# A new order of steps, all stores on SyncE and wider empty matmuls in an RWKV-5 attention with a squared-ReLU feed-forward

## The chip, the core and the metric

The kernel runs on one core of one Trainium2 chip. Its metric is the device time of one execution in microseconds (us). In this kernel TensorE (PE) does matrix products into the accumulators in PSUM, VectorE (DVE) and ScalarE (ACT) work element by element and read those accumulators, GpSimd (POOL) works element by element on data in SBUF and issues some DMAs, and SyncE (SP) only issues DMAs. Each engine works through its own list of instructions in order; waits between engines are semaphores.

## What is computed

The input is r, k, v of shape [4 batches, 8 heads, 768 steps, 48], a decay w and a bonus u per head and channel, and two feed-forward weights, [384, 2048] and [2048, 384]. Per head a state of 48 x 48 runs over time, and its output, with the heads side by side, goes through a feed-forward with a squared ReLU:

```python
for t in range(S):
    cur = einsum('bhd,bhe->bhde', u * k[t], v[t])
    y[t] = einsum('bhd,bhde->bhe', r[t], state + cur)
    state = w * state + einsum('bhd,bhe->bhde', k[t], v[t])
x = y.transpose(0, 2, 1, 3).reshape(B * S, H * D)      # 3072 x 384
out = square(maximum(x @ w_in, 0)) @ w_out             # 3072 x 384
```

## The kernel before

The 3072 rows are cut into 24 chunks of 128 rows. Chunk i belongs to batch i % 4 and is the (i // 4)th of its batch, so chunks 0 to 3 begin the four batches. Inside a chunk the recurrence is written as matrix products with powers of the decay (tables Wkhat and Wt2) on k and r; between chunks it goes through a state per batch (S0W). The steps of chunk i, with their names in the order list:

- `ld.r.i`, `ld.k.i`, `ld.v.i` load 192 KB each. `rh`, `kh` scale r and k to bf16 (lines 338, 335); `P0`, `P1`, `du`, `dv` make the bonus term (341, 345, 348, 353); `vb` casts v.
- Scaled r and k are turned, either by PE (`T`, line 362, copied out by `Tc` on ACT) or by a DMA transpose on SP (`XB`, line 368).
- `A` (line 375) makes the scores, `Bm` (383) masks them, `Y` (391, 393) makes the chunk's output in PSUM, `xs` (410) adds the bonus, `U` (402) is the chunk's share of the state, `S0`, `ts`, `S` (417, 420, 423) update the state.
- The result is turned again, by PE (`X`, 428, copied by `xTc`) or by DMA (`xX`, 435).

The chunks form 13 groups, 0 and 1 with one chunk, 2 to 12 with two (chunks 4 and 5 are group 2, and so on). The feed-forward works on a group: `F1.g.s` (line 444) is one PSUM bank of the first product for group g, `re` (452 on ACT, 454 on DVE) the ReLU of that bank, `sq` (459 on ACT; 461 or 463 on DVE) its square, `F2.i.q` (471) a quarter of the second product for chunk i, and `os.i` and `out.i` (503) copy and store its result. `F1` uses two PSUM banks in turn. `F2c` (485) is the second product of chunk 22 alone, in two halves of columns.

The weights come in pieces. Of w_in there are eight (W1_0 to W1_7, 384 KB each): `lW.0.s` loads piece s into one of four staging buffers wsa (line 323), `cW.0.s` casts it to bf16, on ACT (259) or POOL (261). Piece 2 comes by `W.0.2`, a DMA from POOL that casts on its way (332), and so do the four pieces of w_out (`W.1.q`). A bank `F1.g.s` of groups 0 and 1 needs pieces 2s and 2s+1: `F1.0.2` needs pieces 4 and 5.

`Z.n.b` (line 494) issues n empty matmuls on the identity into bank b, while PE has no data yet.

The whole order is written out by hand in ORDER: one entry per step, `name.indices:engine/buffers`. The program walks through the list once and issues each step on the engine named (P, A, D, G for POOL, S for SP). So the order of the entries of one engine is that engine's program order, and the choice of engine and of buffers stands there too. A step waits for what it reads and for the last readers of the buffer it writes; SP and POOL hold back everything behind a DMA that waits.

## Time and profile before

| what | value |
|---|---|
| median of 3 runs | 174.68 us (174.6 to 174.76) |
| the profiled execution itself | 175.31 us |
| its span, first to last instruction | 173.5 us |
| granted TensorE clock | 1.00 of full speed over the span |
| PE busy | 162.7 us (94%), 1805 matmuls |
| DVE, ACT, POOL busy | 127.8 us, 118.0 us, 91.2 us |
| HBM read and written | 20.46 MB, 4.72 MB |

The span starts with the first instruction of the program; 1.8 us of the profiled execution lie outside it. In rows of the timeline the first number is the start in us from the beginning of the span, the second the duration; "x24" says how many instructions are merged, and the brackets give the idle time before the first of them with what ended it. In groups by line the numbers behind the bar are the busy time, the mean duration of one in ns, and the idle time of the engine before them. Rows of waits give the total, the number of waits and the longest one. Rows on a DMA queue give packets, megabytes and the share of the 16 DMA engines' time. A DMA issue tells how long its queue's sequencer was held and, in the list of issues, the median time until the data had landed.

### The profile page before, as it was taken

How to read it: one execution, taken by the hardware profiler on the slowest of the kernel's cores; microseconds unless marked ns; L12 is line 12 of the kernel's file. 1: busy time of each engine (PE TensorE's matmuls, PEld its weight loads, DVE VectorE, ACT ScalarE, POOL GpSimd, SP SyncE). 2: the span in 40 equal slices, each digit the busy share in tenths (PEclk: the TensorE clock that was granted, in tenths of full speed). 3: DMA queues.
4: the chain of work that ended last, by engine and by line, in shares of the span. 5: the costliest groups of instructions: out<-in, count | busy, mean ns of one | idle time of the engine just before them, and what ended most of it. 6: DMA issues, size and time to landing. Idle time of an engine off the chain costs nothing.

```text
span 173.5 us, 4580 instructions
## 1 busy us (share of the span) xinstructions
PE 162.7 (94%) x1805; PEld 126.7 (73%) x1805; DVE 127.8 (74%) x241; ACT 118.0 (68%) x220; POOL 91.2 (53%) x113
## 2 busy tenths in 40 slices
PE   3979579999999999999999999999999999999992
...
GB/s 98 221 240 278 195 244 194 196 211 215 140 229 210 203 236 154 230 211 178 201 216 173 238 127 183 204 133 209 193 232 135 95 37 26 159 0 91 49 62 74
DMA packets 104788, 29.14 MB, mean 168 GB/s; under 512 B 98008, under 2 KB 104288, under 8 KB 104768
## 3 DMA queue, kind: packets, MB, share of 16 engines
...
q10 hardware_dynamic: 152, 0.14, 0.2%
...
HBM read 20.46 MB, written 4.72 MB: 145 GB/s over the span
## 4 chain that ended last, share of the span: by engine, by line
PE 76%; DMA 11%; SPq 8%; issue 1%; ACT 1%; POOL 1%; DVE 0%; POOLq 0%; ACTq 0%
PE bank L471 33%; PE bank L444 31%; DMA ldk<-in_k_dram 7%; SPq L319 7%; DMA wsa<-in_moe_w_in_dram 3%; PE bank L375 3%; PE bank L393 2%; PE bank L391 2%; PE bank L402 2%; SPq L323 2%; PE bank L485 2%; PE bank L428 1%; PE bank L362 1%; ACT rkT L259 1%; POOL urow L217 0%
## 5 line engine op out<-in xcount | busy, mean ns | idle before, releaser
L444 PE MATMUL bank<-xT,W 128*128 128x256 bf16 (+1 forms) x624 | 74.0, 264 | 1.7 <-POOL W L261 1.3
L471 PE MATMUL bank<-W,hq 128*128 128x384 bf16 x368 | 69.9, 326 | 0.0
L444 PEld LDWEIGHTS <-W 128*128 128x128 bf16 x624 | 55.6, 98 | 12.2 <-POOL W L261 1.6
L452 ACT ACTIVATE hr<-bank 128x512 bf16<-128x512 f32 x78 | 45.7, 596 | 25.6 <-PE bank L444 24.5
L471 PEld LDWEIGHTS <-hq 128*128 128x128 bf16 x368 | 34.5, 98 | 17.6 <-DVE hq L461 0.3
L459 ACT ACTIVATE hq<-hr 128x512 bf16<-128x512 bf16 x77 | 45.6, 625 | 1.9 <-DVE hr L454 1.7
L383 DVE TENSOR_TENSOR Bm<-bank,maskJT 128x512 bf16<-128x512 f32 x48 | 31.0, 681 | 2.7 <-PE bank L375 2.1
L454 DVE TENSOR_SCALAR hr<-bank 128x512 bf16<-128x512 f32 x18 | 12.3, 689 | 16.0 <-PE bank L444 15.9
L345 POOL TENSOR_TENSOR P<-P,ub 128x384 f32<-128x384 f32 x16 | 17.5, 1095 | 12.4 <-DVE P L341 12.3
L341 POOL TENSOR_TENSOR P<-ldr,ldk 128x384 f32<-128x384 f32 x14 | 14.3, 1027 | 11.4 <-DMA ldr<-in_r_dram 6.1
L410 DVE TENSOR_TENSOR xs<-bank,dv 128x384 bf16<-128x384 f32 x24 | 12.8, 549 | 4.9 <-PE bank L393 2.7
L338 POOL TENSOR_TENSOR rk<-ldr,Wt 128x384 bf16<-128x384 f32 x12 | 12.1, 1013 | 7.7 <-DMA ldr<-in_r_dram 7.6
L335 POOL TENSOR_TENSOR rk<-ldk,Wkhat 128x384 bf16<-128x384 f32 x10 | 10.5, 1061 | 7.5 <-DMA ldk<-in_k_dram 5.4
L348 DVE TENSOR_REDUCE du<-P 128x8 f32<-128x384 f32 x24 | 12.9, 543 | 1.6 <-POOL P L345 1.5
L353 POOL TENSOR_TENSOR dv<-ldv,du 128x384 f32<-128x384 f32 x14 | 12.3, 882 | 3.2 <-DVE du L348 3.2
L259 ACT COPY os<-bank 128x384 f32<-128x384 f32 (+1 forms) x17 | 7.9, 473 | 8.0 <-PE bank L471 4.7
L494 PE MATMUL bank<-identity 128*128 128x128 bf16 x139 | 10.4, 240 | 2.7 <-POOL identity masks.py:199 2.7
L494 PEld LDWEIGHTS <-identity 128*128 128x128 bf16 x139 | 9.4, 110 | 2.9 <-POOL identity masks.py:199 2.7
L393 PE MATMUL bank<-vb,Bm 128*128 128x48 bf16 x192 | 10.9, 183 | 0.2 <-ACT xT L259 0.2
L259 ACT CAST vb<-ldv 128x384 bf16<-128x384 f32 x16 | 8.1, 508 | 4.1 <-DMA ldv<-in_v_dram 4.1
L375 PE MATMUL bank<-rkT 48*128 48x128 bf16 x192 | 8.2, 218 | 2.5 <-ACT rkT L259 1.7
L259 ACT COPY rkT<-bank 128x1024 bf16<-128x1024 bf16 x7 | 7.1, 1011 | 4.4 <-PE bank L362 4.4
(64 smaller groups left out, 174.7 us busy)
## 6 DMA issues: line engine op xcount, KB each, us to landing
ldk<-in_k_dram SPq DMA_DIRECT2D x24, 192.0 KB, 3.8
ldr<-in_r_dram SPq DMA_DIRECT2D x24, 192.0 KB, 3.7
ldv<-in_v_dram SPq DMA_DIRECT2D x24, 192.0 KB, 4.0
...
out_dram<-os SPq DMA_DIRECT2D x13, 192.0 KB, 3.0
out_dram<-os POOLq DMA_DIRECT2D x10, 192.0 KB, 3.2
...
rkT<-rk SPq DMA_TRANSPOSE x17, 3.7
```

Source lines behind the costliest of these rows:

```text
L259: e.copy(o, a)
L341: e.tensor_mul(P0b[slot[f"P{i}"]], loaded("r", i), loaded("k", i))
L345: e.tensor_mul(t, t, ub)
L348: e.tensor_reduce(dub[slot[f"dv{i}"]], P0b[slot[f"P{i}"]], axis=mybir.AxisListType.X, op=ALU.add)
L375: e.matmul(heads(bank(f"bA{i}{h}"), 128)[:, hc, :], t[p0 : p0 + D, HP + hc, :], t[p0 : p0 + D, hc, :], start=True, stop=True, skip_group_c ...
L383: e.tensor_mul(Bmb[slot[f"Bm{i}{h}"]], heads(bank(f"bA{i}{h}"), 128), mask_b)
L393: e.matmul(y[:, hc, D * h : D * (h + 1)], m[h][:, hc, :], vb[:, 2 * hc + h, :], start=(c == 0), stop=True, skip_group_check=True,)
L444: e.matmul(hp[:, fi, :], W1[f // 2][:, c, 128 * (f % 2) : 128 * (f % 2 + 1)], xt[:, c, :], start=(c == 0), stop=(c == CCH - 1), skip_group ...
L452: e.activation(hr, hp, AF.Relu)
L459: e.activation(hq, hr, AF.Square)
L471: e.matmul(bank(f"bO{i}", "bO")[:, 0:d_model], hqb[slot[f"hq{g},{f // m}"]][:, at : at + L], W2[q][:, f % 4, :], start=(f == 0), stop=(f = ...
L494: e.matmul(banks[b][:, 0:128], identity, identity, start=True, stop=True, skip_group_check=True)
```

## The change

ORDER is written anew from its first entry to its last, with the same steps. Three more things differ: all 23 whole-chunk stores are issued by SP (ten came from POOL before), `ld.v.3` is issued by POOL instead of SP, and the empty matmuls are issued four at a time as one matmul of 512 columns. What the order list holds up to the second product of the early groups, and at its end:

```diff
-ld.k.2:S/0 w:A tab:A shw:D ld.k.1:S/1 u:S ld.r.1:S/0 Z.48.4:P Z.4.5:P logw:A Wk:A/0 kh.1:D/0 ld.k.0:S/2 P0.1:D/0 WtS:A
-ld.r.0:S/1 Wt:A/1 rh.1:D T.1:P/0 kh.0:D/1 P0.0:G/1 shu:D P1.1:G ld.r.2:S/2 P0.2:G/2 Z.8.4:P ld.k.3:S/3 rh.0:D kh.2:D/2
-ld.r.3:S/3 Tc.1:A/0 rh.2:D P1.0:G Z.16.5:P P0.3:G/3 kh.3:D/3 T.2:P/1 A.1:P/2/3 du.1:D/0 ld.v.1:S/0 Z.13.4:P vb.1:G/0
-Bm.1.0:D/0 Tc.2:A/1 rh.3:D Z.6.5:P T.0:P/0 Bm.1.1:D/1 Tc.0:A/2 ld.v.0:S/1 du.0:D/1 A.0:P/2/1 T.3:P/3 WkS:A vb.0:G/1
-Z.6.4:P Bm.0.1:D/2 Y.1:P/0 Z.22.5:P lW.0.6:S/0 dv.1:G dv.0:G lW.0.0:S/1 Bm.0.0:D/3 wc:S xs.1:D/0 cW.0.6:A lW.0.1:S/2
-lW.0.7:S/3 A.2:P/1/2 Z.16.4:P Bm.2.1:D/4 P1.2:G P1.3:G ld.v.2:S/2 cW.0.1:G cW.0.0:A du.2:D/2 cW.0.7:G Tc.3:A/3 X.1:P/0
-du.3:D/3 Y.0:P/2 xs.0:D/1 xTc.1:A/0 dv.2:G ld.v.3:S/3 vb.2:A/2 A.3:P/3/2 X.0:P/0 vb.3:A/3 WLcol:A Bm.3.0:D/5 Bm.2.0:D/0
-xTc.0:A/1 F1.1.3:P/1 W.0.2:G U.1:P/3 re.1.3:A/0 F1.1.0:P/0 Y.2:P/1 Bm.3.1:D/1 re.1.0:A/1 lW.0.5:S/0 W.1.0:G dv.3:D
-lW.0.4:S/2 Y.3:P/0 xs.3:D/2 F1.0.0:P/1 xs.2:D/3 lW.0.3:S/1 cW.0.5:A W.1.1:G F1.0.3:P/0 X.3:P/2 re.0.0:A/2 sq.1.0:A0/0
-X.2:P/0 xTc.3:A/0 cW.0.4:G U.2:P/1 re.0.3:D/3 W.1.2:G F1.0.2:P/1 cW.0.3:G WLm:G ld.r.4:S/4 F1.1.2:P/0 xTc.2:A W.1.3:G
...
+Z.48.4:P w:A ld.r.0:S/0 ld.r.1:S/1 tab:A shw:D Z.8.5:P u:S ld.k.1:S/0 Z.13.4:P shu:D ld.v.1:S/0 ld.k.0:S/1 P0.1:D/0
+ld.k.2:S/2 Z.6.5:P logw:A P0.0:G/1 Wk:A/0 kh.1:D/0 Wt:A/1 P1.1:D rh.1:D kh.0:D/1 T.1:P/0 Tc.1:A/0 rh.0:D ld.r.3:S/2
+Z.16.4:P T.0:P/1 A.1:P/2/3 ld.v.0:S/1 ld.k.3:S/3 vb.1:A/0 kh.2:D/2 du.1:D/0 rh.3:D/3 Bm.1.1:D/0 Tc.0:A/1 vb.0:A/1
+A.0:P/0/3 kh.3:D ld.r.2:S/3 rh.2:D lW.0.1:S/0 ld.v.2:S/2 Z.22.5:P T.3:P/1 Tc.3:A/2 T.2:P/1 P1.0:G Bm.0.0:D/1 wc:S
+lW.0.7:S/1 Bm.1.0:D/2 dv.1:G Y.1:P/0 Z.16.4:P du.0:D/1 P0.2:G/2 P0.3:G/3 xs.1:D/0 Tc.2:A/3 X.1:P/2 Bm.0.1:D/3 P1.2:G
+vb.2:A/2 A.2:P/0/1 cW.0.7:A Bm.2.0:D/4 A.3:P/3/0 lW.0.6:S/2 cW.0.1:G Bm.2.1:D/5 ld.v.3:G/3 du.2:D/2 xTc.1:A/0 Z.4.5:P
+W.0.2:G dv.0:G dv.2:G Y.0:P/1 P1.3:G Bm.3.0:D/2 Bm.3.1:D/0 Z.6.4:P cW.0.6:A F1.1.3:P/1 vb.3:G/3 xs.0:D/1 Y.2:P/2 X.0:P/3
+lW.0.0:S/3 lW.0.5:S/1 re.1.3:D/0 cW.0.0:A W.1.0:G lW.0.4:S/0 lW.0.3:S/2 du.3:D/3 WtS:A W.1.1:G ld.r.4:S/4 xTc.0:A/1
+xs.2:D/2 WLcol:A cW.0.4:G F1.1.0:P/0 F1.0.3:P/1 Y.3:P/0 U.1:P/1 re.1.0:A/1 dv.3:D X.2:P/3 ld.k.4:S/4 cW.0.5:A xs.3:D/3
+ld.r.5:S/5 F1.0.0:P/0 X.3:P/2 re.0.3:A/2 sq.1.0:A0/0 re.0.0:D/3 xTc.3:A/0 WLm:G ld.k.5:S/5 sq.0.3:D2/1 xTc.2:A
+sq.0.0:D2/2 U.0:P/0 sq.1.3:D2/3 F1.0.2:P/1 re.0.2:A/4 ld.k.7:S/6 F1.1.2:P/0 re.1.2:A/5 F1.2.1:P/1 ld.v.4:S/4 re.2.1:A/1
...
-F2.21.2:P F2.20.0:P/0 re.12.2:A/2 sq.12.2:D2/29 F1.12.5:P/1 F1.12.4:P/0 F2.21.3:P re.12.5:D/0 out.19:S re.12.4:D/4
-os.21:D/3 sq.12.1:D2/6 F1.12.7:P/1 sq.12.3:A0/3 sq.12.6:A0/5 F2.20.1:P re.12.7:A/2 F2.23.0:P/1 sq.12.7:D1/8 F2.23.1:P
-out.21:S sq.12.5:A0/2 F2.20.2:P out.17:G F2.20.3:P sq.12.4:D2/0 F2.23.2:P os.20:A/1 F2.23.3:P F2c.22.1:P/0 os.23:A/3
-out.20:S out.10:G F2c.22.0:P/1 os.22.0:A/0 out.22.0:A os.22.1:D out.23:S out.22.1:S
...
+sq.12.4:D2/25 F2.20.3:P F1.12.1:P/0 sq.12.3:D2/12 F2.21.3:P F1.12.7:P/1 re.12.1:A/4 re.12.7:A/0 os.21:D/3 out.18:S
+F1.12.6:P/0 re.12.6:A/3 os.20:A/0 sq.12.6:A0/2 sq.12.1:D2/8 sq.12.7:D1/1 F2.23.0:P/0 out.19:S F2.23.1:P F2.23.2:P
+F2.23.3:P os.23:A/2 out.20:S F2c.22.1:P/1 F2c.22.0:P/0 out.21:S os.22.0:A/0 os.22.1:D out.16:S out.23:S out.22.1:S
+out.22.0:A
```

The empty matmuls:

```diff
         def Z(e, n, b):
-            for _ in range(n):
+            i = identity[:, :]
+            wide = bass.AP(tensor=i.tensor, offset=i.offset, ap=[list(i.ap[0]), [0, 4], list(i.ap[1])])
+            for _ in range(n // 4):
+                o = banks[b].rearrange("p (a b) -> p a b", a=4)
+                e.matmul(o, identity, wide, start=True, stop=True, skip_group_check=True)
+            for _ in range(n % 4):
                 e.matmul(banks[b][:, 0:128], identity, identity, start=True, stop=True, skip_group_check=True)
```

Steps by engine, before and after: DVE 241 and 257 instructions in all, with `P0` 10 and 14, `kh` 14 and 17, `rh` 12 and 18, `sq` from SBUF alone 15 and 28, `re` 18 and 15, `dv` 10 and 6, `S` 10 and 8, `os` 8 and 5; ACT `re` 78 and 81, `sq` 77 and 64; POOL `rh` 12 and 6, `kh` 10 and 7, `P0` 14 and 10, `dv` 14 and 18, stores 10 and 0.

The steps around the end of the weights' arrival, in program order of their engines, before and after:

```
SP before:   ... lW.0.6/0 lW.0.0/1 wc lW.0.1/2 lW.0.7/3 ld.v.2 ld.v.3 lW.0.5/0 lW.0.4/2 lW.0.3/1 ld.r.4 ...
SP after:    ... lW.0.1/0 ld.v.2 wc lW.0.7/1 lW.0.6/2 lW.0.0/3 lW.0.5/1 lW.0.4/0 lW.0.3/2 ld.r.4 ...
POOL before: ... cW.0.1 cW.0.7 dv.2 W.0.2 W.1.0 W.1.1 cW.0.4 W.1.2 cW.0.3 WLm W.1.3 P0.4 rh.7 P0.5 ...
POOL after:  ... cW.0.1 ld.v.3 W.0.2 dv.0 dv.2 P1.3 vb.3 W.1.0 W.1.1 cW.0.4 WLm W.1.2 cW.0.3 W.1.3 rh.4 kh.5 ...
ACT after:   ... vb.2 cW.0.7 xTc.1 cW.0.6 cW.0.0 WtS xTc.0 WLcol re.1.0 cW.0.5 re.0.3 ...
PE before:   ... F1.0.2 F1.1.2 F1.2.1 F1.2.5 U.3 F1.2.4 F1.2.7 U.0 F1.1.1 F1.0.1 F2.0.0 F1.2.2 F2.1.0 F1.2.0
                 F2.1.1 F2.0.1 T.4 F2.1.2 F1.2.3 F2.0.2 A.4 T.5 F2.1.3 ...
PE after:    ... F1.0.2 F1.1.2 F1.2.1 F1.2.4 U.2 F1.2.5 F1.2.7 U.3 F1.0.1 F1.1.1 F2.1.0 F1.2.2 F1.2.0 F2.0.0
                 F1.2.3 F2.1.1 F2.0.1 T.4 F2.1.2 F1.2.6 A.4 F2.0.2 T.5 F2.1.3 ...
```

The number behind a slash is the staging buffer.

More of the change, by code (lines that the diff above doesn't have):

```diff
@@ new lines @@
+F2.8.0:P/1 A.13:P/1/2 A.12:P/3/0 os.7:D/2 sq.5.3:A0/3 ld.v.14:S/5 F1.6.0:P/0 F2.9.0:P/0 sq.5.4:A0/1 vb.12:G/5 out.6:S
+F1.6.6:P/1 Bm.13.0:D/0 sq.5.2:A0/12 Bm.12.0:D/5 kh.16:D/5 re.6.6:A/4 F2.8.1:P dv.12:G S.11:G Bm.13.1:D/2 ld.k.18:S/3
+Bm.12.1:D/3 re.6.0:D/3 F2.9.1:P F1.6.2:P/1 Y.12:P/1 dv.13:G vb.13:A/6 ld.v.17:S/3 Y.13:P/3 xs.12:D/1 F2.9.2:P
+sq.6.0:A0/4 out.7:S sq.6.1:A0/10 xs.13:D/4 du.14:D/3 F1.6.3:P/0 re.6.2:A/5 kh.17:D A.15:P/2/0 re.6.3:A/1 Bm.15.1:D/4
+A.14:P/1/3 F2.8.2:P S.10:D F1.6.4:P/1 xX.12:S/2 U.13:P/0 F1.6.7:P/0 rh.16:D sq.5.6:A0/14 re.6.4:A/3 vb.14:A/4 F2.9.3:P
@@ new lines @@
+re.7.0:A/2 F1.7.4:P/1 F2.11.1:P sq.6.7:A0/17 out.1:S vb.15:A/1 re.7.4:A/4 F1.7.7:P/0 Bm.16.0:D/1 U.14:P/1 Y.15:P/0
+xs.15:D/2 P0.18:G/2 F1.7.2:P/1 ts.14:D/0 Y.17:P/3 xX.15:S P1.17:D S.14:G U.15:P/2 du.17:D/1 ld.r.23:S/1 F2.11.2:P
+re.7.7:A/1 F1.7.3:P/0 ld.r.20:S/6 sq.7.1:A0/21 re.7.3:D/0 out.8:S du.16:D/4 vb.16:D/0 kh.19:G/6 sq.7.0:A0/18 ld.k.23:S/0
+ld.k.21:S/2 F2.10.1:P F2.11.3:P F2.10.2:P F1.7.5:P/0 rh.20:G/4 rh.18:D dv.17:D sq.7.6:A0/16 sq.7.7:D2/20 xs.17:D/0
+xX.17:S/1 F2.10.3:P dv.16:D U.17:P/0 rh.19:D re.7.2:A/5 os.11:A/1 F1.8.5:P/1 re.7.5:A/2 sq.7.3:A0/22 P0.19:D/4
```

130 lines of the change are left out of this document (60 added, 70 removed).

## Prediction

> **What bounds the kernel now.** I read the page's first two parts, then the waits of PE, then the timeline at the places that these name, then the DMA queues there.
>
> ```profile
> span 173.5 us, 4580 instructions
> PE 162.7 (94%) x1805; PEld 126.7 (73%) x1805; DVE 127.8 (74%) x241; ACT 118.0 (68%) x220; POOL 91.2 (53%) x113
> PE   3979579999999999999999999999999999999992
> ```
>
> PE is busy in every slice from the seventh on. What it waits for:
>
> ```profile
> PE bank L494 <- POOL identity masks.py:199: 2.7, 1, 2.7
> PE bank L375 <- ACT rkT L259: 1.7, 2, 1.1
> PE bank L444 <- POOL W L261: 1.3, 2, 0.8
> PE bank L375 <- DVE xs L410: 0.8, 1, 0.8
> PE bank L362 <- DVE rk L335: 0.4, 1, 0.4
> PE bank L444 <- DVE hr L454: 0.2, 1, 0.2
> PE bank L393 <- ACT xT L259: 0.2, 1, 0.2
> ```
>
> These 7.3 us are all the waits of the span, and the timeline has the last two that count here:
>
> ```profile
> 24.20 0.33 PE L402 MATMUL bank<-vb,rk 128*128 128x96 bf16 x4
> 25.38 1.51 PE L444 MATMUL bank<-xT,W 128*128 128x128 bf16 x24 [0.85 <-POOL W L261]
> ...
> 38.88 0.62 PE L362 MATMUL bank<-identity,rk 128*128 128x128 bf16 x8 [0.42 <-DVE rk L335]
> ```
>
> The row at 25.38 is F1.0.2 with F1.1.2 behind it, held 0.85 us by the cast of a weight piece; the one at 38.88 is T.5, held 0.42 us by the scaled k of chunk 5. After it PE never waits until its last matmul. The set of steps on PE does not change, so the end moves with exactly two things: when PE starts its unbroken run, and which waits come into that run. All PE work that stands before F1.0.2 is the same in both orders but for U.0 in place of U.2, equal in cost. So I compare the start of F1.0.2.
>
> **The start, step by step.** F1.0.2 needs pieces 4 and 5 of w_in, and the last link is the cast cW.0.4 on POOL.
>
> ```profile
> GB/s 98 221 240 278 195 244 194 196 211 215 140 229 210 203 236 154 230 211 178 201 216 173 238 127 183 204 133 209 193 232 135 95 37 26 159 0 91 49 62 74
> ```
>
> ```profile
> 12.71 0.98 SPq L323 DMA_DIRECT2D wsa<-in_moe_w_in_dram  x2
> 19.23 0.42 SPq L323 DMA_DIRECT2D wsa<-in_moe_w_in_dram  x1
> ...
> 14.93 0.90 ACT L259 CAST W<-wsa 128x768 bf16<-128x768 f32 x1 [1.63 <-DMA wsa<-in_moe_w_in_dram]
> ...
> 18.27 0.86 POOL L261 CAST W<-wsa 128x768 bf16<-128x768 f32 x1 [0.51 <-DMA wsa<-in_moe_w_in_dram]
> 24.46 0.86 POOL L261 CAST W<-wsa 128x768 bf16<-128x768 f32 x1 [1.03 <-DMA wsa<-in_moe_w_in_dram]
> ```
>
> Now: lW.0.1, first of the two issued at 12.71, lands for its cast at 18.27. That cast ends at 19.13 and frees buffer 2, so lW.0.4 is issued at 19.23, its cast starts at 24.46 and ends at 25.32, and F1.0.2 goes at 25.38. From issue of the piece to start of the cast it is 5.2 us.
>
> After: behind wc, as lW.0.1 is now, SP issues lW.0.7; eleven chunk loads and one piece stand ahead of it, before ten and two, so I take the same landing, about 18.2. Its cast is on ACT, 0.90 there (row at 14.93), so it ends at 19.1, and only then may lW.0.5 use buffer 1. lW.0.4 stands behind lW.0.5 in SP's order although its own buffer is long free: it goes half a us later, at 19.65. Plus 5.2 plus 0.86 is 25.7 if nothing else runs. But lW.0.1 becomes the first piece of all, in the place of the one that is cast at 14.93, and behind its cast, at 16 to 17.5, POOL now issues ld.v.3 and W.0.2, some 3 to 4 us ahead of the row at 20.98; and the DMA queue of POOL takes turns with SP's:
>
> ```profile
> 20.98 0.93 POOL L332 DMA_DIRECT2D W<-in_moe_w_in_dram  x1
> ```
>
> ```profile
> ## 3 DMA queue, kind: packets, MB, share of 16 engines
> q0 software_dynamic: 1315, 1.47, 94.2%
> q1 hardware_dynamic: 1456, 0.28, 26.2%
> ```
>
> The second fence is the stretch from 26 to 35 us: POOL's queue (q0) and SP's (q1) moved about as many packets, but POOL's are larger, and SP's loads crept: 0.28 MB in 9 us. So what POOL sends earlier is paid by the pieces. W.0.2 reads 0.39 MB, and in the sixth slice of the span (21.7 to 26.0 us), in which the last pieces come, the queues move 244 GB/s, so it costs them up to 1.6 us. POOL itself holds cW.0.4 too: it now stands behind vb.3, which needs the landing of ld.v.3. I take 0.7 of the 1.6: F1.0.2 at 26.4, **1.0 us later**. Bounds: if the pieces land early, PE's own work ends at about 24.7 (the U.2 row above ends at 24.5, plus 0.2 for the copies in its way), 0.7 earlier than now; with all 1.6 us and half a us of vb.3 it is 27.5, 2.1 later.
>
> The Trainium skill (DMA: Bandwidth & Descriptors, Queues, rings and completion order) says that each engine goes round-robin between queue rows packet by packet; the 1315 and 1456 packets above agree. By that rule alone, a small-packet ld.v.3 on POOL takes little and W.0.2 its full share, which would put F1.0.2 at 27.3.
>
> **The wait at 38.88 goes: minus 0.42.** T.5 waits for kh.5, and that for ld.k.5, which lands at 38.2:
>
> ```profile
> 38.26 0.56 DVE L335 TENSOR_TENSOR rk<-ldk,Wkhat 128x384 bf16<-128x384 f32 x1 [0.21 <-DMA ldk<-in_k_dram]
> ```
>
>  In the new order one more F1 stands between F1.0.2 and T.5 (twelve F1 and six F2, before eleven and six), 0.65 us by the rows of the chain of waits:
>
> ```profile
> 160.38 1.31 PE bank L444 x12
> 162.99 4.55 PE bank L471 x28
> ```
>
> From 25.38 to 38.88 without the 0.42 is 13.1; from 26.4 with one F1 more T.5 comes at 40.1. kh.5 moves to POOL, 1.06 us there (row below), so it is ready at 39.3 with the same landing. No wait; if ld.k.5 landed 0.8 us later than now, it would begin to come back.
>
> **The rest.** Wide empty matmuls: 139 become 33 of 512 columns and seven of 128, all in the first 20 us and ahead of the same weights.
>
> ```profile
> 7.65 1.50 PE L494 MATMUL bank<-identity 128*128 128x128 bf16 x24
> ```
>
> ```profile
> L471 PE MATMUL bank<-W,hq 128*128 128x384 bf16 x368 | 69.9, 326 | 0.0
> ```
>
> Four narrow ones take 0.25 us by the first row. Matmuls of 384 columns pass at 0.163 each where 28 stand in a row (162.99 above), which scales to 0.22 for 512 columns; alone they take the 0.33 of the second row. So a wide one costs 0.22 to 0.33, and 33 of them from 1.0 us less to 2.6 us more. All lie in gaps that end with a landing or a cast: I take 0. Stores:
>
> ```profile
> L503 POOL DMA_DIRECT2D out_dram<-os x10 | 5.8, 582 | 4.4 <-DVE os L261 2.5 <-ACT os L259 2.0
> out_dram<-os SPq DMA_DIRECT2D x13, 192.0 KB, 3.0
> out_dram<-os POOLq DMA_DIRECT2D x10, 192.0 KB, 3.2
> ```
>
> POOL loses ten issues of 0.58 and waits in front of them, 10.2 us in all; nothing on PE hangs on that, so 0. SP gains ten. A store that waits for its copy holds every load behind it on SP, but in the list each stands 1.5 us or more of PE work behind its copy: 0, up to a load's 3.8 us if one is missed. At the end, buffer 0 of os goes from chunk 20 to 22, so os.22 now waits for out.20. By the rows below os.20 ends 1.1 us after the last F1, PE has 5.2 us left from there (four F2, and F2c.22 at 0.65 us for every 1536 columns), and 1.1 + 0.4 for the issue + 3.0 is 4.5: 0, up to 0.4 if the store lands as slowly as the slowest.
>
> ```profile
> L452 ACT ACTIVATE hr<-bank 128x512 bf16<-128x512 f32 x78 | 45.7, 596 | 25.6 <-PE bank L444 24.5
> L259 ACT COPY os<-bank 128x384 f32<-128x384 f32 (+1 forms) x17 | 7.9, 473 | 8.0 <-PE bank L471 4.7
> ```
>
> ```profile
> DMA to landing us min/median/max: 1.7/3.0/4.1
> ```
>
>  POOL has rh.4, kh.5 and kh.9 in PE's path, 0.5 us more each than on DVE; XB.8 now stands behind XB.9. These steps have about a us to spare each; I put **0.2** for new waits, 0 to 1.3.
>
> Sum: 1.0 - 0.42 + 0.2 = +0.8 on the profiled execution, 175.31 to 176.1. That one lies 0.63 above the median, the same work; on the median, 174.68 to **175.5**.
>
> **Rivals.** (1) *The pieces land early.* lW.0.7 has fewer bytes of pieces ahead, and SP has no other load behind it until 19 us. It decides if that piece lands by 17.5 and POOL's transfers cost nothing: then F1.0.2 starts at 25.0 (0.9 + 0.55 + 5.2 + 0.86 behind the landing), the sum is -0.4 - 0.42 = -0.8: 173.9. For it: the casts wait for landings now, not for engines. Against: the 5.2 us are the shortest way of a piece in the trace. (2) *Nothing shows.* F1.0.2 at 25.8 and no wait at T.5 cancel: 174.7. (3) *DVE becomes the bound*, slower still.
>
> ```profile
> 61.60:114.60 53.00, 53.00 (x590) 40.75 (x587) 45.15 (x81) 43.32 (x86) 37.00 (x41) 1.00 0.97 196
> ```
>
> ```profile
> L341 DVE TENSOR_TENSOR P<-ldr,ldk 128x384 f32<-128x384 f32 x10 | 6.3, 627 | 0.8 <-DMA ldk<-in_k_dram 0.8
> L335 DVE TENSOR_TENSOR rk<-ldk,Wkhat 128x384 bf16<-128x384 f32 x10 | 6.8, 681 | 0.8 <-DMA ldk<-in_k_dram 0.7
> L338 DVE TENSOR_TENSOR rk<-ldr,Wt 128x384 bf16<-128x384 f32 x8 | 4.4, 549 | 2.0 <-DMA ldr<-in_r_dram 2.0
> L463 DVE TENSOR_TENSOR hq<-hr 128x512 bf16<-128x512 bf16 x15 | 7.2, 483 | 1.4 <-ACT hr L452 1.4
> L335 POOL TENSOR_TENSOR rk<-ldk,Wkhat 128x384 bf16<-128x384 f32 x10 | 10.5, 1061 | 7.5 <-DMA ldk<-in_k_dram 5.4
> ```
>
> From the first mask of chunks 8 and 9 to that of 18 and 19, DVE is busy 45.15 of 53 us with 79 steps. In the new list it has 99: seven more squares (3.4), four more P0 (2.5), four more kh (2.7), three more rh (1.6) and two others (0.9), 11.1 us, so 56.3 in a stretch that holds 55.2 us of PE work. The price is 1.1 us on top of the forecast, 176.6. It decides only if the durations count in full; back-to-back ones overlap by 0.08, which takes 8 us off and leaves room. That PE never waited while DVE was at 85% speaks against. The kh row (mean 681, shortest 542) shows that some wait inside; the Trainium skill (SBUF — State Buffer, Who interferes with whom) says that a DVE instruction with two SBUF inputs and a GpSimd one that reads SBUF exclude each other. By that rule eighteen more such steps at the row's 0.14 pay 2.5 us, and the rival would give 179.1 with nothing hidden.
>
> **How the numbers follow.** Forecast 0.50, 175.0 to 176.5; rival 1 0.20, 173.4 to 174.3; rival 2 0.18, within 0.35 us of now; rival 3 0.12, 176.6 and above. 0.2% of 174.68 is 0.35 us, about what a measurement can tell from no change. Faster 0.20, same 0.20 (rival 2 and the forecast's edge), slower 0.60. The range runs from 173.9, in the middle of rival 1, to 177.0, which takes in rival 3 without the rule's price.
>
> **What would show it.** Right: F1.0.2 starts near 26.4 behind a wait of 1 us or more for the cast on POOL, lW.0.4 is issued near 19.6 behind the cast of piece 7, T.5 waits for nothing, PE has no wait over 0.3 us after it, and the time from its last matmul to the end of the span is as now. Wrong: F1.0.2 at or before 25.4, or waits on PE after 40 us (for DVE between 60 and 115, or for a DMA transpose before A.8) that add up to more than the start does.

## The result and the profile after

Over 20 runs of each the changed kernel takes **174.49 us** (median; 173.47 to 176.52) and the kernel before 175.39 (174.49 to 180.75). The ratio is **0.9944**, 95% interval 0.9917 to 0.9971: faster by 0.56%, where the forecast was slower by 0.5%. Three more sets, each on a chip of its own and run with the experiments, gave 0.9964 [0.9928, 1.0000], 0.9998 [0.9963, 1.0032] and 0.9976 [0.9942, 1.0009]; the mean of the four is 0.3%, and two of them can't be told from no change. The gain is small. A median here is over all runs, while a ratio and its interval come from the fast runs alone, those within 1.5% of their kernel's fastest in the set, so the two need not agree (one set below has 0.9998 where its medians give 0.9946). The three runs shown before (174.68) lay at the low end of their kernel; the profiled execution of before (175.31) is a typical one. On that base my +0.8 meant 176.1, so the miss is 1.6 us, not the 1.0 between 175.5 and 174.49.

The profiled execution of after takes 174.47 us, 0.84 less than that of before. Its first part and its waits on TensorE (columns: us in total, times, longest):

```profile
span 172.6 us, 4392 instructions
PE 162.2 (94%) x1706; PEld 121.6 (70%) x1706; DVE 127.9 (74%) x257; ACT 114.3 (66%) x214; POOL 77.3 (45%) x94
PE   3987769999999999999999999999999999999992
```

```profile
PE bank L498 <- POOL identity masks.py:199: 2.7, 1, 2.7
PE bank L445 <- POOL W L262: 1.3, 1, 1.3
PE bank L363 <- ACT rkT L260: 1.1, 1, 1.1
PE bank L376 <- ACT rkT L260: 0.8, 1, 0.8
PE bank L376 <- DVE Bm L384: 0.6, 1, 0.6
PE bank L429 <- DVE xs L411: 0.6, 1, 0.6
```

GpSimd has lost 14 us of work, and no wait on `rk` (T.5) or on `hr` is left; the one for the last weight piece has grown from 0.85 to 1.3. The timeline of TensorE says what these are worth. After:

```profile
25.82 3.01 PE L445 MATMUL bank<-xT,W 128*128 128x128 bf16 x36 [1.30 <-POOL W L262]
28.67 0.33 PE L403 MATMUL bank<-vb,rk 128*128 128x96 bf16 x4
28.91 1.47 PE L445 MATMUL bank<-xT,W 128*128 128x256 bf16 x12
30.21 0.33 PE L403 MATMUL bank<-vb,rk 128*128 128x96 bf16 x4
30.41 0.77 PE L445 MATMUL bank<-xT,W 128*128 128x128 bf16 x11
...
39.15 0.61 PE L363 MATMUL bank<-identity,rk 128*128 128x128 bf16 x8
...
166.53 2.80 PE L486 MATMUL bank<-W,hq 128*128 128x128 bf16 x32
```

Before, the rows that were not shown yet:

```profile
27.08 1.48 PE L444 MATMUL bank<-xT,W 128*128 128x256 bf16 x12 [0.19 <-DVE hr L454]
28.40 0.33 PE L402 MATMUL bank<-vb,rk 128*128 128x96 bf16 x4
28.77 1.47 PE L444 MATMUL bank<-xT,W 128*128 128x256 bf16 x12
30.07 0.33 PE L402 MATMUL bank<-vb,rk 128*128 128x96 bf16 x4
30.32 0.89 PE L444 MATMUL bank<-xT,W 128*128 128x128 bf16 x13
...
167.38 2.80 PE L485 MATMUL bank<-W,hq 128*128 128x128 bf16 x32
```

Four numbers come out of these rows.

- **Start**: F1.0.2 at 25.82 in place of 25.38: +0.44.
- **From there the same steps in both** (F1.0.2, F1.1.2, four F1 of 256 columns, two U) take to 30.32 before, 4.94 us, and to 30.41 after, 4.59: -0.35. The old list loses 0.19 of it where an F1 waits for the bank that a relu still reads (first row); the rest lies in stops too short to be listed as a wait.
- **F1.0.2 to T.5**: 13.33 after, 13.50 before, which has one F1 (0.65) less in it. So 0.82 is saved: the 0.35, the wait of 0.42 at T.5, and 0.05.
- **T.5 to the end of the last matmul**: 130.18 after (166.53 + 2.80 - 39.15), 131.30 before. The F1 that went ahead accounts for 0.65; 0.47 is saved in stops of which none is listed as a wait. The two largest are 0.16 us inside Y.5 (near 45.0 us) and 0.11 us ahead of an F2 (123.57).

Sum: 0.44 - 0.82 - 0.47 = -0.85, and the span is 0.9 shorter. The time behind the last matmul is 3.3 in both.

### The profile page after: what moved, and what is told of

The parts are those of the page before. It is cut to its first block, busy times and chain, and to the rows that moved or that the text cites. A ratio compares the mean times of both kernels' runs of the same rounds, so it can differ in the third digit from the quotient of the medians.

```text
span 172.6 us, 4392 instructions
## 1 busy us (share of the span) xinstructions
PE 162.2 (94%) x1706; PEld 121.6 (70%) x1706; DVE 127.9 (74%) x257; ACT 114.3 (66%) x214; POOL 77.3 (45%) x94
## 3 DMA queue, kind: packets, MB, share of 16 engines
q0 software_dynamic: 1808, 1.97, 6.6%
## 4 chain that ended last, share of the span: by engine, by line
PE 89%; ACT 4%; DMA 3%; POOL 1%; issue 1%; SPq 0%; POOLq 0%; ACTq 0%
PE bank L445 36%; PE bank L472 35%; PE bank L498 4%; PE bank L376 4%; DMA ldr<-in_r_dram 3%; PE bank L394 2%; PE bank L392 2%; ACT rkT L260 2%; PE bank L403 2%; PE bank L363 2%; PE bank L486 2%; PE bank L429 1%; ACT W L260 1%; ACT vb L260 1%; POOL W L262 1%
## 5 line engine op out<-in xcount | busy, mean ns | idle before, releaser
L453 ACT ACTIVATE hr<-bank 128x512 bf16<-128x512 f32 x81 | 47.8, 597 | 32.5 <-PE bank L445 31.1
L460 ACT ACTIVATE hq<-hr 128x512 bf16<-128x512 bf16 x64 | 38.3, 628 | 0.4 <-DVE hr L455 0.4
L354 POOL TENSOR_TENSOR dv<-ldv,du 128x384 f32<-128x384 f32 x18 | 15.4, 860 | 22.8 <-DVE du L349 13.4
L464 DVE TENSOR_TENSOR hq<-hr 128x512 bf16<-128x512 bf16 x28 | 12.8, 479 | 3.6 <-ACT hr L453 3.6
L342 POOL TENSOR_TENSOR P<-ldr,ldk 128x384 f32<-128x384 f32 x10 | 9.9, 997 | 7.4 <-DMA ldk<-in_k_dram 4.7
L498 PE MATMUL bank<-identity 128*128 128x512 bf16 x33 | 10.6, 468 | 2.7 <-POOL identity masks.py:199 2.7
L336 POOL TENSOR_TENSOR rk<-ldk,Wkhat 128x384 bf16<-128x384 f32 x7 | 7.3, 1040 | 7.8 <-DMA ldk<-in_k_dram 7.5
L339 DVE TENSOR_TENSOR rk<-ldr,Wt 128x384 bf16<-128x384 f32 x14 | 8.1, 582 | 3.4 <-DMA ldr<-in_r_dram 3.4
L394 PEld LDWEIGHTS <-Bm 128*128 128x128 bf16 x192 | 9.6, 96 | 0.7 <-issue 0.2
L421 DVE TENSOR_TENSOR ts<-bank,S0W 128x384 f32<-128x384 f32 x16 | 8.7, 549 | 1.8 <-PE bank L403 1.7
```

The lines of the kernel that those rows point to most:

```text
L354: e.tensor_mul(dvb[slot[f"dv{i}"]], loaded("v", i), t)
L394: e.matmul(y[:, hc, D * h : D * (h + 1)], m[h][:, hc, :], vb[:, 2 * hc + h, :], start=(c == 0), stop=True, skip_group_check=True,)
L453: e.activation(hr, hp, AF.Relu)
L460: e.activation(hq, hr, AF.Square)
L498: e.matmul(o, identity, wide, start=True, stop=True, skip_group_check=True)
```

## The experiments

My theory after the result: the terms of the sum are the right ones, but (a) the new list runs with no stop at all behind F1.0.2, where the old one loses something in every execution, and (b) the wide empty matmuls or the stores brought the start forward. Rivals: the small edits alone make the gain; the gain is all in the start; it is only a matter of scatter.

All runs in one table. Each median stands beside that of the kernel before in the same set (12 runs of each kernel, 6 of e6 and e15; 23 to 35 of the kernel before). The next columns are from the trace of one execution of each: start of F1.0.2, how long T.5 was held, and the time from T.5 to the end of the last matmul. The last column counts runs with a mean granted clock under 0.995, of which more below. e3, e10, e11 and e16 change the start itself. One of the six runs of e15 took 912.5 us at a full clock; nothing on record says why, and its ratio rests on the other five.

```
run  edit                          median / before   ratio [95%]               F1.0.2  T.5 held  T.5 to end  low clock
     before, as profiled           175.39            1                         25.38   0.42      131.30      30 of 151 (five sets)
     after, as profiled            174.49 / 175.39   0.9944 [0.9917, 0.9971]   25.82   0         130.18      5 of 20
e5   after again                   175.10 / 175.65   0.9964 [0.9928, 1.0000]   26.57   0         130.18      2 of 12
e9   after again                   174.95 / 175.90   0.9998 [0.9963, 1.0032]   25.50   0         130.94      3 of 12
e18  after again                   175.07 / 175.32   0.9976 [0.9942, 1.0009]   25.66   0         130.18      3 of 12
e7   after, narrow Z               176.06 / 175.65   0.9995 [0.9955, 1.0036]   26.60   0.57      130.28      6 of 12
e14  after, narrow Z               176.46 / 176.01   0.9983 [0.9940, 1.0025]   26.44   0         130.18      6 of 12
e12  after, quarter Z              174.54 / 175.90   0.9977 [0.9937, 1.0017]   25.77   0         130.19      0 of 12
e15  after, quarter Z              174.64 / 176.01   0.9896 [0.9850, 0.9943]   26.19   0         130.19      0 of 6
e17  after, no Z                   174.52 / 175.32   0.9956 [0.9924, 0.9988]   26.09   0         130.20      0 of 12
e11  after, three Z more           174.97 / 175.90   1.0002 [0.9964, 1.0040]   26.69   0         130.22      0 of 12
e8   after, stores on GpSimd       174.80 / 175.65   0.9934 [0.9899, 0.9969]   25.55   0         130.18      1 of 12
e3   after, piece 4 first          175.17 / 176.14   0.9973 [0.9939, 1.0007]   26.75   0         130.32      1 of 12
e10  after, W.0.2 late             175.07 / 175.90   0.9986 [0.9943, 1.0029]   24.67   0.51      131.11      1 of 12
e16  e12, W.0.2 late, kh.5 on DVE  175.21 / 176.01   0.9955 [0.9922, 0.9989]   25.52   0         131.63      0 of 12
e1   before, wide Z, stores on SP  175.79 / 176.14   1.0004 [0.9965, 1.0043]   24.79   1.28      131.81      2 of 12
e13  before, quarter Z             177.06 / 176.01   1.0020 [0.9978, 1.0061]   24.97   0         132.18      5 of 12
e4   before, F1.2.6 ahead of T.5   175.96 / 176.14   1.0012 [0.9970, 1.0054]   26.04   0         131.45      2 of 12
e2   e1's start, rest of after     175.76 / 176.14   0.9988 [0.9947, 1.0028]   25.16   0.64      131.56      1 of 12
e6   after's start, rest of before 177.96 / 175.65   1.0112 [1.0065, 1.0159]   26.21   0         133.67      1 of 6
```

**The small edits in the old list, and the stores in the new one.** e1 is the kernel before with `ORDER` unchanged but for `out.1 .3 .4 .7 .8 .9 .10 .14 .15 .17` from `:G` to `:S`, and the new Z:

```
-            for _ in range(n):
+            i = identity[:, :]
+            wide = bass.AP(tensor=i.tensor, offset=i.offset, ap=[list(i.ap[0]), [0, 4], list(i.ap[1])])
+            for _ in range(n // 4):
...
```

> The kernel before with two of the three edits and its old order: the ten stores of GpSimd's queue go to SyncE at their old places in the list, and the empty matmuls are 512 columns wide. Theory order: neither edit moves the end, the gain is all in the order. Ratio to before 0.999 to 1.001, F1.0.2 at 25.4 us, T.5 held 0.4 us, last matmul ending at 170.2. Rival stores: GpSimd free of ten issues and of its waits, and 1.9 MB fewer on its queue, give the gain. Ratio 0.994, last matmul ending near 169.3. Rival clock: the clock is granted later behind the wide empty matmuls (7.7 us in the changed kernel, 6.1 before) and costs the start; F1.0.2 at 25.8.

The time is that of before, as the theory of the order has it, but not for its reason: the start did come forward. From TensorE's timeline of e1:

```profile
24.79 1.51 PE L446 MATMUL bank<-xT,W 128*128 128x128 bf16 x24 [0.84 <-POOL W L263]
...
39.20 0.62 PE L364 MATMUL bank<-identity,rk 128*128 128x128 bf16 x8 [1.28 <-DVE rk L337]
...
168.21 2.80 PE L487 MATMUL bank<-W,hq 128*128 128x128 bf16 x32
```

F1.0.2 starts 0.59 earlier, and T.5, which is gated by the landing of k of chunk 5, is held 1.28 us instead of 0.42; behind it 0.5 more is lost. In this trace the gain at the start does not come through, and the ratio shows none. e8 is the changed kernel with the same ten stores back on GpSimd's queue:

```
-... out.4:S ... out.3:S ... out.7:S ...
+... out.4:G ... out.3:G ... out.7:G ...
```

> The changed kernel with the ten stores back on GpSimd's queue, at their places in its list. Theory none: same time as the changed kernel in this set within 0.2%, no new wait on TensorE over 0.3 us. Rival: GpSimd, which waits for the copy in front of each store, gives its scaled k and r and its tables late; waits of TensorE for them return after 40 us, 0.5 us or more in all, ratio to before 0.997 or over.

Behind F1.0.2 TensorE has no listed wait, as in after, and 0.9934 beside 0.9964 in one set tells no difference. The queue of the stores costs nothing that these runs can tell, as predicted.

**One F1 ahead of T.5 in the old list** (e4):

```
-... du.4:D/4 T.5:P/0 F2.1.3:P P0.5:G/0 sq.2.0:D1/11 F1.2.6:P/1
+... du.4:D/4 F1.2.6:P/1 T.5:P/0 F2.1.3:P P0.5:G/0 sq.2.0:D1/11
```

> The kernel before with F1.2.6 ahead of T.5 on TensorE, three steps earlier, and nothing else moved. It fills the 0.42 us that T.5 is held. Theory next in line: the copy of T.5 on ScalarE stands behind the cast of v of chunk 4, which starts at 39.76 when that load lands; so the copy ends at 41.2 as now, TensorE comes to A.5 0.4 us earlier and waits there instead. T.5 held 0, A.5 held 0.3 to 0.5, ratio 0.999 to 1.001. Rival: the wait goes for good, ratio 0.9975, last matmul ending at 169.7.

T.5 waits for nothing, A.5 waits 0.19 for its copy, and no gain is seen; but 0.42 us would be a ratio of 0.9976, which lies inside the interval, so these runs can't exclude it. Behind T.5 this list has the same steps as the new one and takes 131.45 in place of 130.18. That the time of the wait moved down there is not shown: the old list loses as much behind T.5 without this edit (e1 and e13, below).

**The grafts.** e2 takes the old list up to F1.0.2 and from there the steps in the new order; e6 the reverse. Four and eight buffer numbers had to change. Both have the wide empty matmuls: the expectation of e2 says narrow, but its kernel has the new Z, and its trace 1706 matmuls as after has, not 1805. The seam of e2, as a change to the kernel before:

```
 ... U.2:P/1 re.0.3:D/3 W.1.2:G F1.0.2:P/1
-cW.0.3:G WLm:G ld.r.4:S/4 F1.1.2:P/0 xTc.2:A W.1.3:G ...
+ld.r.4:S/4 ld.k.4:S/4 ld.r.5:S/5 WLm:G ld.k.5:S/5 ...
```

> The old order up to and with F1.0.2 (narrow empty matmuls), and from there the steps in the new order, with the stores on SyncE; four buffer numbers differ, where the new one is still taken. Theory sum: the terms add. F1.0.2 at 25.4 as before, no wait at T.5, and the 0.8 us of small stalls gone as in the changed kernel: 0.4 us better than that one, ratio to before 0.991 to 0.993, last matmul ending at 168.9. Rival tied: the rest is only good behind the start that it was searched with, because the loads of chunk 5 now land as late as before (38.2 us) or later: T.5 is held 0.3 to 0.6 us again, ratio 0.994 to 0.998.

> The changed kernel's order up to and with F1.0.2, and from there the old order with its stores on GpSimd's queue; eight buffer numbers differ. Theory sum: start as in the changed kernel (F1.0.2 at 25.8 us) and the small stalls of the old rest (0.8 us); at T.5 no wait to 0.3, because ld.k.5 stands in the new start and lands at 37.4; ratio to before 0.998 to 1.001. Theory scatter: what varies is the order of the loads up to F1.0.2, which is the new one here, so the ratio is that of the changed kernel, 0.994 to 0.996, and the middle half of the runs lies within 0.8 us. Rival rest: all of the gain, scatter too, comes from the steps after F1.0.2: ratio 1.000 and a middle half of 1 us or more.

Both theories of the sum fall. e2 starts at 25.16 and then holds T.5 for 0.64, as its rival said, and loses 1.4 us behind it; its ratio, 0.9988, lies a little above the rival's range too. e6 is outside every range that was named and the slowest of all; its largest stop comes 30 us behind the graft, at a transpose of the mixed rows, for an addition on VectorE (TensorE's timeline of e6):

```profile
58.46 0.75 PE L430 MATMUL bank<-identity,xs 128*128 128x128 bf16 x5 [1.27 <-DVE xs L412]
```

Neither list's rest runs clean behind the other's start. How much of this the changed buffers cost was not parted from it.

**Does the new rest run clean?** e5, e9 and e18 are the changed kernel again.

> The changed kernel as it is, to stand beside its own variants on one chip. Theory scatter: the first set showed the kernel before at 174.2 to 178.6 us at a full clock, so its landings vary, and the changed order has more slack against them; ratio to before 0.990 to 0.996, middle half of its runs within 0.6 us, that of before within 1 to 2.2. Theory sum: a fixed number of small waits less; ratio 0.9944 and the same scatter as before.

> The changed kernel as it is, beside its variants on one chip. Theory clean run: from T.5 to the end of the last matmul it takes 130.2 us again, whatever the start (130.19, 130.19 in its two traces so far; the old order lost 0.5 and 1.0 us behind T.5), so its time is F1.0.2's start plus 148.9 us, and its spread that of this start: middle half of the runs within 0.7 us. Ratio to before 0.992 to 0.998. Rival: the rest varies as much as the start; the stretch behind T.5 is 130.5 or longer.

> The changed kernel as it is, beside the form with no empty matmuls. Both theories: ratio of medians to before 0.993 to 0.997 over all runs, F1.0.2 at 25.5 to 26.6 behind a stop of 0.9 to 1.7 us, one run in four or five at a clock under 0.995, and 130.2 us from T.5 to the end of the last matmul.

They change nothing, so there is no diff. e9 missed its 130.2 us and e18 its ratio and the length of its stop (2.00 us). In e5 F1.0.2 starts 0.75 later than in the first trace, and everything behind it is as late and no later (TensorE's timeline):

```profile
26.57 1.12 PE L445 MATMUL bank<-xT,W 128*128 128x128 bf16 x17 [1.71 <-POOL W L262]
...
39.90 0.61 PE L363 MATMUL bank<-identity,rk 128*128 128x128 bf16 x8
...
167.28 2.80 PE L486 MATMUL bank<-W,hq 128*128 128x128 bf16 x32
```

13.33 and 130.18 again. Of the thirteen traces with the new list unchanged behind F1.0.2 (stores apart), eleven take 130.18 to 130.32 from T.5 on; e9 takes 130.94, with a wait of 0.4 at the scores of a later chunk, and e10, in which W.0.2 goes later, 131.11. A clean run of the old list would be 130.18 + 0.65 = 130.83; its three traces take 131.30, 131.81 and 132.18. So the old list loses 0.47, 0.98 and 1.35 us behind T.5, not always at the same places, and the new one next to nothing in eleven of thirteen. With the 0.35 us ahead of T.5 and the wait there, that is the gain; the start takes part of it back. Which of the moved steps makes the new list run clean was not found. The clean run is likely also why scatter falls: in the set of e5, of the runs at a clock of 0.996 or more, the middle half of before lies between 175.19 and 176.41, that of after between 174.60 and 175.18.

**The empty matmuls.** e7 and e14 are the new list with the old Z (139 of 128 columns), e12 and e15 have 40 of 128 columns, e17 has none (every `Z` taken out of the list). The edit of e12, to the changed kernel; that of e7 is the diff of e1, read backwards:

```
             for _ in range(n // 4):
-                o = banks[b].rearrange("p (a b) -> p a b", a=4)
-                e.matmul(o, identity, wide, start=True, stop=True, skip_group_check=True)
+                e.matmul(banks[b][:, 0:128], identity, identity, start=True, stop=True, skip_group_check=True)
```

> The changed kernel with its empty matmuls 128 columns wide again, as many columns in all. Theory none: they lie in gaps that end with a landing or a cast; same time as the changed kernel in this set within 0.2%, F1.0.2 at 25.8 give or take 0.5 us. Rival clock: the narrow ones get the full clock earlier (6.1 us before, 7.7 in the changed kernel), up to 0.5 us faster. Rival queue: 132 instructions instead of 33 hold TensorE's queue, 0.3 to 1 us slower.

> The changed kernel with 139 narrow empty matmuls, beside the quarter form on one chip. Theory fetch: median 0.4 to 0.8% behind the quarter form, a fetch between 20 and 25 us, F1.0.2 at 26.3 to 27.0, a third or more of its runs at a clock under 0.995. Rival: the first set of it was chance; within 0.2% of the quarter form.

> The changed kernel with as many empty matmuls as it has, but 128 columns wide: 40 instructions and a quarter of the columns. It parts the two sides of the wide form, fewer instructions and longer ones. Theory fetch: with 139 narrow ones TensorE fetches its instructions earlier, and a fetch of 16 KB falls into 20 to 25 us, among the pieces of w_in (it did in all three traces with that many, and in none with 40); with 40 instructions of either width it stays out, and F1.0.2 starts at 25.5 to 26.6 as in the unchanged one; same time within 0.2% unless the clock comes late. Rival columns: it is the busy time that counts, which keeps the clock; then this one is as slow as the narrow form, 0.3 to 0.5% behind the unchanged one, or slower, with several runs at a low clock.

> The changed kernel with 40 empty matmuls of 128 columns, on one chip with the narrow form and the old order. Theory fetch: ratio to before 0.991 to 0.996, no run or one at a clock under 0.995, from T.5 to the last matmul 130.2 us. Rival: 1.000 as the narrow form.

> The changed order with no empty matmuls at all (40 instructions fewer than the quarter form). Theory instructions: what counts is how few instructions stand ahead of F1.0.2; TensorE's own steps run at half speed and end at about 25.5 us, when the last piece is cast anyway; F1.0.2 at 25.5 to 26.3 with hardly a stop ahead of it, no run or one under a clock of 0.995, median 0.1 to 0.4% below the changed kernel of this set. Rival columns: without them the clock comes later still, F1.0.2 goes at half speed for 1 to 3 us, and the time is 0.5 to 1.5 us over the changed kernel's.

With the narrow form no gain can be told: the ratios are 0.9995 and 0.9983, and the medians stand 0.4 us above before. Only part of that is the start. F1.0.2 starts at 26.60 and 26.44, against 25.82, 26.57, 25.50, 25.66 and 25.55 (e8) with the wide one, 0.7 later in the mean (26.52 and 25.82). The old start shows the same: 25.38 (before) and 26.04 (e4) with 139 empty matmuls, 24.79 (e1), 24.97 (e13) and 25.16 (e2) with 40, again 0.7 apart in the mean. At a clock of 0.996 or more the medians of e7 and e5, from one set, are 175.44 and 174.97, and those of e14 and e15 175.08 and 174.64, so some 0.45 us. At that clock e14 is still 0.9 us below before (175.98), while e7 is level with it (175.52): in e14 it is the other six runs, at a low clock, that take the gain away. TensorE's timeline of e14:

```profile
26.44 1.23 PE L446 MATMUL bank<-xT,W 128*128 128x128 bf16 x19 [1.94 <-POOL W L263]
...
39.77 0.61 PE L364 MATMUL bank<-identity,rk 128*128 128x128 bf16 x8
...
167.15 2.80 PE L487 MATMUL bank<-W,hq 128*128 128x128 bf16 x32
```

Its rest is clean (13.33 and 130.18): only the start is late (in e7 T.5 is held 0.57 as well). A part of what the instructions do there may be seen in the DMA queues from 20 to 25 us, in which the last pieces land; of e14, then of e9 with the wide form:

```profile
q1 hardware_dynamic: 1473, 1.14, 76.2%
q0 software_dynamic: 400, 0.20, 31.5%
q8 instruction: 1, 0.02, 1.1%
```

```profile
q1 hardware_dynamic: 2061, 1.31, 85.1%
q0 software_dynamic: 173, 0.15, 18.8%
```

A fetch of instructions (0.02 MB in one packet) lies among the loads of e14, and SyncE's queue (q1) moves less. Such a fetch is there in all four traces with 139 empty matmuls (before, e4, e7 and e14), and in none of the fifteen with 40 or 43. But e5, with no fetch there, moved only 1.11 MB on q1 and started as late, and e17, with no empty matmul, has one there, starts F1.0.2 at 26.09 and is the quickest in its set.

Most of the 0.7 is in fact older than 20 us. Piece 4 is issued at 19.39 and 18.86 in e7 and e14 and at 17.75 to 19.21 (mean 18.62) in the five wide traces; piece 7 at 13.45 and 13.53, against 11.86 to 12.71. But it is nearly as late in e3 (13.34) and e11 (13.00), whose lists are unchanged up to there, so two narrow traces are few to go by. All four traces with 139 have an earlier fetch too, near 11 us, where no other trace has one, and in e14 SyncE's issues are slow there. Its timeline, of e14 and then of e9:

```profile
10.48 1.60 SPq L321 DMA_DIRECT2D ldv<-in_v_dram  x1
12.21 1.27 SPq L306 DMA_DIRECT2D wcol<-in_w_dram  x2
```

```profile
10.21 0.49 SPq L320 DMA_DIRECT2D ldv<-in_v_dram  x1
10.83 0.99 SPq L305 DMA_DIRECT2D wcol<-in_w_dram  x2
```

So an earlier start with fewer empty matmuls is what the means of a few traces show; that the fetches are the way to it is argued from their times alone.

The other part is the clock. The profiled execution of e18 has a mean clock of 0.987; its timeline, and its stretch from 24 to 30 us:

```profile
25.66 2.04 PE L445 MATMUL bank<-xT,W 128*128 128x128 bf16 x19 [2.00 <-POOL W L262]
...
40.46 0.61 PE L363 MATMUL bank<-identity,rk 128*128 128x128 bf16 x8
```

```profile
24.00:30.00 6.00, 4.34 (x37) 3.88 (x38) 1.95 (x4) 3.88 (x8) 3.90 (x6) 0.72 1.24 212
```

After the same stretch of the first trace of after:

```profile
24.00:30.00 6.00, 4.69 (x62) 4.13 (x60) 3.64 (x5) 5.02 (x10) 4.90 (x7) 1.00 1.22 210
```

(The last three columns are granted clock, DMA share and GB/s.) Behind a stop of 2.00 us the clock falls to 0.72 over these 6 us (it is 0.50 from 25.88 to 29.29) and F1.0.2 to T.5 takes 14.80 in place of 13.33: 1.47 us. A mean clock under 0.995 stands in 12 of 24 runs of the new list with the narrow form, in 13 of 56 of the unchanged one, and in none of 42 with the quarter form, no Z or a filler. That each of them had such a stop is not shown: only e3 and e18 were traced in that state. The filler (e11) is three more empty matmuls:

```
-... sq.1.3:D2/3 F1.0.2:P/1 ...
+... sq.1.3:D2/3 Z.12.6:P F1.0.2:P/1 ...
```

> The changed kernel with three more empty matmuls of 512 columns (0.65 us) ahead of F1.0.2, in a bank that is free there. Theory clock: runs in which TensorE stands still for 2 us or so ahead of F1.0.2 lose the full clock for some microseconds (a trace with 1.97 us there has 0.88 as its mean clock from 26 to 40 us, and ends 1.5 us later); with the filler the stop is 0.65 us shorter, and fewer runs show a mean clock under 0.995: 0 or 1 of 12, where the unchanged one had 5 of 20 and 2 of 12. Median as the unchanged one within 0.2%, slowest runs 1 to 2 us better. Rival: the filler itself is in the way and the time is 0.2 to 0.6 us longer.

As expected the low clock goes; the median does not move (174.97 and 174.95). In the quarter form TensorE's own steps begin at about half speed (eight transposes take 1.06 us at 8.90, and 0.61 in after at 9.20) and end at 25.8, so F1.0.2 follows with hardly a stop. Timeline of e12, and that of e17, where TensorE does nothing for 7.3 us:

```profile
25.77 0.45 PE L445 MATMUL bank<-xT,W 128*128 128x128 bf16 x5
```

```profile
7.32 0.61 PE L364 MATMUL bank<-identity,rk 128*128 128x128 bf16 x4 [7.32 <-DVE rk L337]
...
26.09 3.01 PE L446 MATMUL bank<-xT,W 128*128 128x128 bf16 x36 [1.57 <-POOL W L263]
```

The empty matmuls bring this list nothing that these runs can tell. But the old list with the quarter form (e13; it has 40, not 37) is no faster than before either:

> The kernel before, old order and stores as they were, with 37 empty matmuls of 128 columns in place of 139. Theory fetch: no instruction fetch among the pieces (10 to 15 and 20 to 25 us), F1.0.2 at 24.5 to 25.2 in place of 25.4; but the old order then waits at T.5 for k of chunk 5, 0.8 to 1.4 us, and loses 0.4 to 1 us behind it as in its other traces, so that the median gains 0.1 to 0.3% and the spread stays wide (middle half of the runs 1 us or more). Rival fetch is all: the median gains 0.5% as the change did, and the spread is that of the changed kernel.

It starts at 24.97, T.5 waits for nothing, and it loses 1.35 us behind T.5: part of the expectation is wrong (no wait at T.5, and a median above that of before). Fewer instructions alone do not make the gain. Why 5 of its 12 runs have a low clock is open; its trace has no stop ahead of F1.0.2.

**The last piece.** Three edits to the changed kernel: e3 swaps two loads, e10 moves W.0.2, and e16 is e10 with the quarter form and one more step moved.

```
 e3
-lW.0.0:S/3 lW.0.5:S/1 re.1.3:D/0 cW.0.0:A W.1.0:G lW.0.4:S/0 lW.0.3:S/2
+lW.0.0:S/3 lW.0.4:S/0 lW.0.5:S/1 re.1.3:D/0 cW.0.0:A W.1.0:G lW.0.3:S/2
 e10 and e16
-W.0.2:G dv.0:G dv.2:G Y.0:P/1 P1.3:G ... F1.1.3:P/1 vb.3:G/3
+dv.0:G dv.2:G Y.0:P/1 P1.3:G ... F1.1.3:P/1 vb.3:G/3 W.0.2:G
 e16
-ld.v.6:S/5 P0.5:D/0 Tc.4:A/4 F2.1.2:P kh.5:G
+ld.v.6:S/5 kh.5:D P0.5:D/0 Tc.4:A/4 F2.1.2:P
```

> The changed kernel with the load of piece 4 of w_in ahead of that of piece 5 on SyncE. Its buffer is free from 15.98 us on, when the cast of piece 1 ends; that of piece 5 only from 18.38 on. Theory order of issue: piece 4 goes at 16.0 and lands by 22, piece 5 goes at 18.4 as now and lands at 24.0 to 24.4; with its cast of 0.9 on ScalarE F1.0.2 starts at 25.0 to 25.3, 0.5 to 0.8 us earlier, ratio to before 0.990 to 0.992. Rival bytes: up to there the queues are full and the last of the same pieces lands at the same 24.8, whichever it is: F1.0.2 at 25.8, ratio 0.994 as the changed kernel.

> The changed kernel with the load of piece 2 (W.0.2, on GpSimd's queue, 0.39 MB) four steps later, behind the copy of v of chunk 3 at 21.3 us in place of 17.0. Theory bytes: what this load moves before 21 us is taken from pieces 4 and 5; piece 4 lands 5.2 us behind its issue, not 6.0, F1.0.2 starts 0.5 to 0.8 us earlier than in the unchanged one of this set, and so does the end; ratio 0.996 of it. Rival: the queues are idle enough between 17 and 21 us for it; no change within 0.2%. Rival later: its bytes now meet those of w_out and of chunks 4 and 5, and T.5 is held 0.3 us or more, so that the end is the same or later.

> The quarter form with piece 2 (W.0.2) behind the copy of v of chunk 3 on GpSimd, and the scaled k of chunk 5 on VectorE ahead of the product of chunk 5 (0.56 us there, 1.30 on GpSimd). Theory both: F1.0.2 at 24.7 as in e10 and no wait at T.5, for k of chunk 5 is ready 0.5 to 0.7 us earlier; T.5 at 38.2, the end 0.5 to 0.9 us earlier than the quarter form, ratio 0.996 of it. Rival next: the products and masks behind it on VectorE come 0.5 us later and TensorE waits for the masks of chunk 4 ahead of Y.4; same time as the quarter form within 0.2%.

e3 met neither of its expectations. In its trace piece 5, now the last, lands at 25.3 for a cast on ScalarE, F1.0.2 waits for a relu that stands behind that cast, and the stop of 1.97 us cost the clock: whichever piece goes last, it is late. e10 gives a price for W.0.2, from one trace (its timeline):

```profile
24.67 1.51 PE L446 MATMUL bank<-xT,W 128*128 128x128 bf16 x24 [0.47 <-POOL W L263]
...
38.67 0.62 PE L364 MATMUL bank<-identity,rk 128*128 128x128 bf16 x8 [0.51 <-POOL rk L337]
```

Piece 4 lands 4.1 us behind its issue instead of 6.2 (e9, of the same set), F1.0.2 starts 0.83 earlier, and then T.5 is held and 0.9 is lost behind it; the end is the same. e16 clears T.5, but F1.0.2 starts at 25.52 and not at 24.7, since TensorE's own slow steps last until then, and TensorE later waits for masks (its timeline):

```profile
44.76 0.22 PE L395 MATMUL bank<-vb,Bm 128*128 128x48 bf16 x2 [0.40 <-DVE Bm L385]
```

By the order of the steps this is Y.5 with the masks of chunk 5, not Y.4 as the rival had it: on VectorE `rh.7` stands ahead of them and sits 1.15 us for its load. So the rival of e10 was right about what is late next, and that of e16 right about the kind of step but not the chunk. The median of e16 is 0.3% above that of the quarter form (175.21 and 174.64).

**Fewer empty matmuls.** The new list with fewer empty matmuls is in its sets 0.2 to 0.3% below the changed kernel (174.54 and 174.95; 174.52 and 175.07 with none). Against before they stand clear of 1 in one set each, 0.9896 [0.9850, 0.9943] (e15, five runs) and 0.9956 [0.9924, 0.9988] (e17), and not in e12's, 0.9977 [0.9937, 1.0017]. Against the changed kernel the difference is within the scatter of 12 runs.

## Why the prediction was wrong, step by step

- **The start of the new order, +1.0: about right.** I put F1.0.2 at 26.4 with no effect of the empty matmuls; with the old ones it starts at 26.60 and 26.44, and the old list's starts with them are 25.38 and 26.04. That the number met is partly luck, since two terms in it were off. In the trace of after piece 7 landed at 16.45, not 18.2, and was cast at 17.50, behind a copy and a cast on ScalarE, so lW.0.4 went at 18.87, not 19.65. And from issue to landing of piece 4 it took 6.0 to 6.9 us in the four traces of the changed kernel, where I had 5.9. The 0.7 for W.0.2 is 0.83 in e10, one trace beside another.
- **The wide empty matmuls, 0: wrong, the first step that failed.** "All lie in gaps that end with a landing or a cast: I take 0." I priced only their time on TensorE, and took it that the gaps' ends stay where they are. The runs show in its place that the landing that ends the last gap comes earlier with 99 instructions fewer: 0.7 us at F1.0.2 between the means of a few traces, in both lists alike, some 0.45 between medians at the full clock, and low clocks in a quarter of the runs and not in half. Without the wide form the new order is no faster than the old one, median 0.4 us over it in both sets (176.06 and 175.65, 176.46 and 176.01), which is where the forecast pointed. By what way the instructions act stays open.
- **The wait at T.5, -0.42: right** in the trace of after, though with the narrow form T.5 is held again in one of two (0.57 in e7). In the old list the wait was 0.42, 1.28 (e1) and 0 (e13). That taking it away alone need not bring time (e4) I had not seen.
- **The rest, +0.2 for new waits: wrong, the second step that failed**, and the larger one: -0.40 ahead of T.5 beside the wait there, and -0.47 behind it (up to 1.35 in other traces of the old list). I looked for new waits in the new list and took the old one's run behind 40 us as unbroken, since the busy digits show nines and the list of waits nothing there. One of the stops was even in the rows that I quoted (0.2 for `hr`), and I set it aside. The time between two rows of the timeline, less the steps between them, would have shown 0.47.
- **Stores 0, the end of the kernel 0: right** (e8; 3.3 us behind the last matmul in both).
- **Rival 3, VectorE as the bound**: did not come. From 61.6 to 114.6 us VectorE is busy 48.62 of 53.00 us in after (45.15 before), and TensorE has no wait there, nor anywhere behind T.5 in that trace.
- **Rival 1** gave a time near the one measured (173.9) by another way: piece 7 did land by 17.5 as it asked, but F1.0.2 was not early. SP did have other loads behind that piece before 19 us, lW.0.6 at 12.66 and lW.0.0 at 13.56.
- **The sum** on the profiled executions should have been +0.44 - 0.82 - 0.47 in place of +1.0 - 0.42 + 0.2.
